# Placing the heads' rows: neighbouring rows against alternating rows

## Chip, cores and metric

The kernel runs on one core of a Trainium2 chip. The metric is the device time of one execution in microseconds. The five engines of the core work from queues of their own, each in order: PE (TensorE, matrix multiplies; PEld is its weight load), DVE (VectorE), ACT (ScalarE), POOL (GpSimd) and SP (SyncE, which here only issues DMAs). [...]

## The reference

A gated linear attention with a complex gate, then a mixture of experts in which each token goes to one expert. Shapes: q, k, v, a_re, a_im are (4, 8, 768, 48): batch, head, token, dimension.

```python
mag = np.sqrt(a_re * a_re + a_im * a_im)
scale = np.minimum(mag, 0.999) / (mag + 1e-06)
a_re_n, a_im_n = (a_re * scale, a_im * scale)
for t in range(S):
    ar, ai = (a_re_n[:, :, t, :, None], a_im_n[:, :, t, :, None])
    new_re = ar * S_re - ai * S_im
    new_im = ar * S_im + ai * S_re
    kv = np.einsum('bhd,bhe->bhde', k[:, :, t], v[:, :, t])
    S_re, S_im = (new_re + kv, new_im)
    y[:, :, t] = np.einsum('bhd,bhde->bhe', q[:, :, t], S_re)

x = y.transpose(0, 2, 1, 3).reshape(3072, 384)
logits = x @ w_gate                      # 8 experts
expert_idx = np.argmax(logits, axis=1)
gate_w = softmax(logits)[expert_idx]
for e in range(8):
    xe = x[expert_idx == e]
    out[expert_idx == e] = gate_w * (np.maximum(xe @ w1[e], 0.0) @ w2[e])
```

## The kernel before

**From gates to a matrix product.** The product of gates from one token to another is the exponential of a difference of running sums of logarithms, with an angle that is a difference of running sums too. So each q and k is multiplied by its own magnitude and by the cosine and the sine of its own angle, and q·k over the 96 rows "48 cosine products, 48 sine products" is the score. A chunk of 128 tokens is then done as ordinary causal attention inside the chunk plus a state carried from chunk to chunk.

**Two layouts.** The gates, queries and keys are worked on in 128 rows with three groups `g` along the row: `BLOCKS` (L25) lists which rows and groups hold which heads and dimensions. Heads 0 to 2 are rows 0 to 47 of the groups 0 to 2, heads 3 to 5 rows 48 to 95; heads 6 and 7 are cut: their dimensions 0 to 31 are rows 96 to 127 of the groups 0 and 1, their dimensions 32 to 47 rows 96 to 111 and 112 to 127 of group 2. The host lays the inputs out so (`_layout`, L797), so all 128 rows work in every elementwise instruction. The matrix multiplies want something else: for each head, 96 rows that hold part 0 (cosine) and part 1 (sine) of its 48 dimensions. That is the tile `hz` (two slots of 384 tokens, q and k of eight heads along the row, rows 96 to 127 zero).

**`front(u)`** (L273) does a unit of 128 to 384 tokens (`UNITS`, L27, ten of them): loads of gates (`AB`) and of q and k (`Z`) on SP (L292), logarithms and exponentials on ACT (L259), running sums as scans on DVE (L314, L325), sine and cosine on ACT, and four products on DVE into `zp`, [128 rows, part, q|k x group x token] (L337 to L345). Then ten DMAs copy `zp` to `hz` (L346 to L362): for each part and each block, rows of `zp` to the rows `part * D + d0` and following of `hz`. They are issued by SP, for the first unit four of them by ACT. There is one `zp`, so the next unit's products wait until these copies have read it.

**`chunk(b, c, full)`** (L369) does one chunk of 128 tokens out of `hz`: transposes of k on PE (L388) copied by ACT to `kt` (L390), scores (L395, `bank<-hz`), the causal mask on DVE into `am` (L399; shown as L172, the helper that issues it), the state's part (L407), the values (L414), the state's update (L422) and the turn to token rows (L430). `route` (L435) chooses experts, and POOL scatters the token rows to DRAM (L490). After all that the experts run (L608 to L670): weights loads on SP (L603, L605), token rows read back (L612), matrix multiplies L639 and L653.

**The order.** Up to the experts no order is written by hand. Each operation is added to a `Plan` (L46) with its engine, an assumed duration, the keys that it reads and writes, and for a DMA a latency `lat` and a wire time `wire`; `run` (L94) simulates the queues, and `order` (L142) tries 36 priorities and takes the shortest. The sequence of instructions in every engine's queue follows from these figures. For the copies into `hz` the wire time is the bytes at 0.213 MB per us (L361).

**The fallback.** If a check of the numbers' range fails at run time, a slow exact version (L686 to L791) runs in place of the result. It uses `BLOCKS` too (L715 to L723). With these inputs it doesn't run.

Of the kernel before, what the change touches and what calls it, by code (L numbers as in the profile page):

```python
# [12 lines left out]
AX = mybir.AxisListType.X  # L13
ALU = mybir.AluOpType
# [3 lines left out]
B, H, S, D = 4, 8, 768, 48  # L18
# [3 lines left out]
DT, FT = DM // 128, F // 128  # L22
G = 3

BLOCKS = ((0, 48, 0, 3, 0, 0), (48, 96, 0, 3, 3, 0), (96, 128, 0, 2, 6, 0), (96, 112, 2, 3, 6, 32), (112, 128, 2, 3, 7, 32))  # L25
TU = 384
UNITS = [(0, 0, 128), (0, 128, 384), (0, 384, 768)] + [(b, t, t + TU) for b in (1, 2) for t in (0, TU)] + [(3, 0, 384), (3, 384, 640), (3, 640, 768)]  # L27
NU = len(UNITS)
# [130 lines left out]
def gateloop_then_moe(ctx, tc, gates, qk, v, wg, w1, w2, out):  # L159
    nc = tc.nc  # L160
# [13 lines left out]
    def const(shape, nm, val=None, dt=FP32):  # L174
        t = consts.tile(shape, dt, name=nm)
        if val is not None:
            nc.gpsimd.memset(t, val)
        return t
# [13 lines left out]
    ident = const([128, 128], "ident")  # L192
# [26 lines left out]
    with ExitStack() as att:  # L219
        ap = att.enter_context(tc.tile_pool(name="ap", bufs=1))  # L220

        def buf(nm, n, shape, dt=FP32):
            return [ap.tile(shape, dt, name=f"{nm}{i}") for i in range(n)]
# [4 lines left out]
        zp, = buf("zp", 1, [128, 2, 2 * G * TU])  # L228
# [6 lines left out]
        hz = buf("hz", 2, [128, 2 * H * TU])  # L235
# [37 lines left out]
        def front(u):  # L273
            b, t0, t1 = UNITS[u]
            T = t1 - t0
# [5 lines left out]
            slot = (2 * b + t0 // TU) % 2  # L281
            sl = slice(0, T)
            a, im, c = bAB[s][:, 0, :, sl], bAB[s][:, 1, :, sl], bC[s][:, :, sl]
# [53 lines left out]
            for part, key, tr in ((1, Sk, si), (0, ("co",), co)):  # L337
                for x, xk, src in ((1, K, kk), (0, Q, qq)):
                    def f(part=part, tr=tr, x=x, src=src):
                        if T == TU:  # L340
                            tt(zp[:, part].rearrange("p (z g t) -> p z g t", z=2, g=G)[:, x], src, tr, ALU.mult)
                        else:
                            o = zp[:, part].rearrange("p (c z g t) -> p z g c t", z=2, g=G, t=128)[:, x, :, 0:nch]
                            tt(o, src.rearrange("p g (c t) -> p g c t", t=128), tr.rearrange("p g (c t) -> p g c t", t=128), ALU.mult)
                    P.add("DVE", dve2(n), f, (xk,) + tuple(key), (("zp", part, x),), port=True)  # L345
            for part in (1, 0):  # L346
                for p0, p1, g0, g1, h0, d0 in BLOCKS:
                    m, r0 = g1 - g0, part * D + d0
                    eng, dma = ("ACT", nc.scalar) if u == 0 and part == 0 and h0 else ("SP", nc.sync)

                    def f(dma=dma, p0=p0, p1=p1, g0=g0, g1=g1, h0=h0, r0=r0, m=m, part=part):
                        o, i = hz[slot][r0:r0 + p1 - p0], zp[p0:p1, part]
                        if T == TU:
                            o, i = o.rearrange("p (z x) -> p z x", z=2), i.rearrange("p (z x) -> p z x", z=2)
                            dma.dma_start(o[:, :, h0 * T:(h0 + m) * T], i[:, :, g0 * T:g1 * T])
                        else:
                            o = o.rearrange("p (c x) -> p c x", x=H * 128)[:, 2 * cl:2 * (cl + nch), h0 * 128:(h0 + m) * 128]
                            dma.dma_start(o, i.rearrange("p (c x) -> p c x", x=G * 128)[:, 0:2 * nch, g0 * 128:g1 * 128])
                    i = P.add(eng, 0.65, f,
                        (("zp", part, 0), ("zp", part, 1)), tuple(("h", slot, cl + x, h, part, d0) for x in range(nch) for h in range(h0, h0 + m)),  # L360
                        lat=1.6, wire=2 * (p1 - p0) * m * T * 4e-6 / 0.213)  # L361
                    moved.setdefault(u, []).append(i)  # L362

        def load_v(b, half):
# [147 lines left out]
        with tc.manual_schedule():  # L512
# [18 lines left out]
            for i in P.order():  # L531
                o = P.ops[i]
# [153 lines left out]
    with tc.If(flag[0] > 0, preferred_fallthrough_block=False), ExitStack() as fs:  # L686
# [4 lines left out]
        v_tok = v.rearrange("b c p (h w) -> (c p) b h w", h=H)  # L691
        x_tok = x_gen.rearrange("(b s) (h e) -> s h b e", b=B, h=H)
        with tc.For_i(0, S // TU) as hi, tc.For_i(0, TU, TB) as j0:
            i0 = hi * TU + j0
            a = fp.tile([128, 2, B, G, TB], FP32, name="fa")
            z_ = fp.tile([128, 2, B, G, TB], FP32, name="fqk")
            for o, src in ((a, gates), (z_, qk)):
                for u in range(2):
                    for b in range(B):
                        nc.sync.dma_start(o[:, u, b], src[b].rearrange("s p u g t -> p s u g t")[:, ds(hi, 1), u, :, ds(j0, TB)])  # L700
            M_ = B * G * TB
            sq = fp.tile([128, 2, M_], FP32, name="fsq")
            mag = fp.tile([128, M_], FP32, name="fmag")
            den = fp.tile([128, M_], FP32, name="fden")
            af = a.rearrange("p u b g t -> p u (b g t)")
            nc.scalar.activation(sq, af, func=ACT.Square)
            tt(mag, sq[:, 0, :], sq[:, 1, :], ALU.add)
            nc.scalar.activation(mag, mag, func=ACT.Sqrt)
            nc.vector.tensor_scalar_add(den, mag, 1e-6)
            nc.vector.reciprocal(den, den)  # L710
            nc.vector.scalar_tensor_tensor(out=den, in0=mag, scalar=0.999, in1=den, op0=ALU.min, op1=ALU.mult)
            tt(af, af, bc(den[:, None, :], [128, 2, M_]), ALU.mult)
            heads = fp.tile([128, G, H], FP32, name="heads")
            nc.gpsimd.memset(heads, 0.0)
            for p0, p1, g0, g1, h0, d0 in BLOCKS:  # L715
                for g in range(g0, g1):
                    nc.vector.tensor_reduce(mag[:, 0:1], ident[:, p0:p1], axis=AX, op=ALU.add)
                    tt(heads[:, g, h0 + g - g0:h0 + g - g0 + 1], heads[:, g, h0 + g - g0:h0 + g - g0 + 1], mag[:, 0:1], ALU.add)
            for t in range(TB):
                vt = fp.tile([128, G, B, D], FP32, name="vt")  # L720
                for p0, p1, g0, g1, h0, d0 in BLOCKS:
                    for g in range(g0, g1):
                        nc.sync.dma_start(vt[p0:p1, g], v_tok[ds(i0 + t, 1), :, h0 + g - g0].to_broadcast([p1 - p0, B, D]))  # L723

                def col(x, u):
                    return bc(x[:, u, :, :, t:t + 1].rearrange("p b g o -> p g b o"), shape)
                z = {}
                for x in range(2):
                    for y in range(2):
                        z[x, y] = fp.tile(shape, FP32, name=f"fz{x}{y}")  # L730
                        for g in range(G):
                            tt(z[x, y][:, g], state[:, x, g], col(a, y)[:, g], ALU.mult)
                kv = fp.tile(shape, FP32, name="kv")
                for g in range(G):
                    tt(kv[:, g], vt[:, g], col(z_, 1)[:, g], ALU.mult)
                tt(state[:, 0], z[0, 0], z[1, 1], ALU.subtract)
                tt(state[:, 1], z[0, 1], z[1, 0], ALU.add)
                tt(state[:, 0], state[:, 0], kv, ALU.add)
                for g in range(G):
                    tt(kv[:, g], state[:, 0, g], col(z_, 0)[:, g], ALU.mult)  # L740
                for g in range(G):
                    nc.tensor.matmul(bank[0][0:H, 0:B * D], lhsT=heads[:, g, :], rhs=kv[:, g].rearrange("p b e -> p (b e)"),
                                     start=(g == 0), stop=(g == G - 1))
                ys = fp.tile([H, B, D], FP32, name="ys")
                nc.vector.tensor_copy(ys.rearrange("h b e -> h (b e)"), bank[0][0:H, 0:B * D])
                for b in range(B):
                    nc.sync.dma_start(x_tok[ds(i0 + t, 1), :, b].rearrange("o h e -> (o h) e"), ys[:, b])
        with tc.For_i(0, NT, 1) as ti:
# [13 lines left out]
            m = fp.tile([128, 1], FP32, name="m")  # L762
# [34 lines left out]
def _layout(name, a):  # L797
    import numpy as _np
    if name in ('q', 'k', 'a_re', 'a_im'):
        z = _np.zeros((B, 128, G, S), a.dtype)  # L800
        for p0, p1, g0, g1, h0, d0 in BLOCKS:
            z[:, p0:p1, g0:g1] = a[:, h0:h0 + g1 - g0, :, d0:d0 + p1 - p0].transpose(0, 3, 1, 2)
        a = z.reshape(B, 128, G, S // TU, TU).transpose(0, 3, 1, 2, 4)
    elif name == 'v':
        a = a.transpose(0, 2, 1, 3).reshape(B, C, 128, DM)
    elif name == 'moe_w_gate':
        z = _np.zeros((128, 4, E), a.dtype)
        for h in range(H):
            z[64 * (h % 2):64 * (h % 2) + D, h // 2, :] = a[h * D:h * D + D]
        a = _np.concatenate([z.reshape(128, 4 * E), a.reshape(4, DT, 32, E).transpose(0, 2, 1, 3).reshape(128, DT * E)], axis=1)  # L810
    elif name == 'moe_w1':
        a = a.reshape(E, 4, DT, 32, F).transpose(0, 1, 3, 2, 4).reshape(E * 128, DT * F)
    else:
        a = a.reshape(E, FT, 128, DM).transpose(0, 2, 1, 3).reshape(E * 128, FT * DM)
    return _np.ascontiguousarray(a)
# [21 lines left out]
```

## Time and profile before

| | |
|---|---|
| median of 6 runs | 581.61 us (577.99 to 583.36) |
| profiled execution | 581.38 us, of which the span of instructions is 579.6 us |
| mean granted TensorE clock | 0.922 |
| PE busy | 476.6 us (82%), 2689 instructions |
| PEld | 322.1 us (56%) |
| DVE busy | 272.5 us (47%), 449 instructions |
| ACT busy | 187.1 us (32%) |
| POOL busy | 115.8 us (20%) |
| DMA | 86.15 MB in 48424 packets, mean 149 GB/s |
| copies `hz<-zp` | 100 issues: 96 by SP, 4 by ACT; 2.6 to 13.1 us from issue to landing, median 5.6 |

How to read the prediction's lines. A line of a stage gives its start and end, its length, then for each engine the busy microseconds and in brackets the number of instructions; then the share of full clock that TensorE was granted, the mean busy share of the 16 DMA engines (it can pass 1 slightly), and the GB/s that they moved. A line of the waits names who waited for whom, then the microseconds in total, the number of waits and the longest. A line of the timeline gives start, length, engine, line, operation, output and input, and in square brackets the idle time before it and what ended it. The shares over the whole span hide that there are two halves: attention up to about 262 us, in which all engines and the DMAs are in use, and the experts from about 280 us on, which are nearly all TensorE.

### The profile page before, as it was taken

To read this page: it belongs to the slowest core of one execution; us is meant where nothing else is said; L and a number is where in the kernel's file an instruction comes from. 1 tells how busy PE (TensorE), PEld (TensorE's weight loads), DVE (VectorE), ACT (ScalarE), POOL (GpSimd) and SP (SyncE) were. 2 spreads that over 40 slices of the span, in tenths; PEclk is the share of its full clock that TensorE was granted. 3 is DMA by queue.
4 is the path that set the end of the run, shared out by engine and by line. 5 is a ranking of instruction groups with operands and counts; after the bars stand their busy time and mean duration, and the time that the engine had idled before them with its cause. 6 is when DMAs were issued, how large, how long until landed. Compare 5 with 4: busy or idle time off the path is not lost. (4 is left out here: it accounts for less than half of the span.)

```text
span 579.6 us, 6981 instructions
## 1 busy us (share of the span) xinstructions
PE 476.6 (82%) x2689; PEld 322.1 (56%) x2689; DVE 272.5 (47%) x449; ACT 187.1 (32%) x261; POOL 115.8 (20%) x116
## 2 busy tenths in 40 slices
PE   0056639778978598991699999999999999999995
PEld 0055529668867487991355555555555555555552
DVE  7788978799998797742221202212022120211011
ACT  6666684668684665540011001000010000000000
POOL 6063111214610821503000002010020100202022
PEclk9975958898979598997699999999999999999999
DMA  8649494969899993787984504546042300401001
GB/s 273 155 170 256 121 207 134 243 180 242 225 255 215 230 207 75 173 341 243 289 145 121 155 15 146 147 135 168 16 152 109 124 15 14 149 0 32 1 36 34
DMA packets 48424, 86.15 MB, mean 149 GB/s; under 512 B 22512, under 2 KB 37904, under 8 KB 46336
## 3 DMA queue, kind: packets, MB, share of 16 engines
q1 hardware_dynamic: 43840, 75.19, 49.3%
q0 software_dynamic: 3328, 9.86, 4.7%
q10 hardware_dynamic: 1216, 0.59, 0.6%
q8 instruction: 23, 0.38, 0.3%
q14 instruction: 17, 0.14, 0.1%
HBM read 54.32 MB, written 13.21 MB: 117 GB/s over the span
## 5 line engine op out<-in xcount | busy, mean ns | idle before, releaser
L639 PE MATMUL bank<-xrt,w1b 128*128 128x448 f32 x384 | 149.5, 546 | 9.3 <-DVE xrt L624 9.3
L653 PE MATMUL bank<-w2b,ht 128*128 128x384 f32 x384 | 127.7, 487 | 0.0
L639 PEld LDWEIGHTS bank<-xrt,w1b 128*128 128x128 f32 x384 | 73.8, 193 | 80.0 <-issue 66.4
L395 PE MATMUL bank<-hz 128*128 128x128 f32 x384 | 65.0, 326 | 59.5 <-DMA hz<-zp 48.5
L653 PEld LDWEIGHTS bank<-w2b,ht 128*128 128x128 f32 x384 | 72.6, 190 | 54.0 <-issue 8.7
L645 ACT ACTIVATE ht<-bank 128x448 f32<-128x448 f32 x32 | 17.4, 543 | 262.7 <-PE bank L639 262.7
L395 PEld LDWEIGHTS bank<-hz 128*128 128x128 f32 x384 | 57.5, 231 | 64.4 <-DVE lend L296 28.7
L586 POOL DMA_INDIRECT out_dram<-yo,gi x24 | 23.5, 978 | 276.7 <-DVE yo L597 243.1
L642 DVE TENSOR_SCALAR ht<-bank 128x448 f32<-128x448 f32 x32 | 19.9, 623 | 114.1 <-PE bank L639 114.1
L597 DVE TENSOR_SCALAR yo<-bank,gi 128x384 f32<-128x384 f32 x24 | 14.8, 618 | 100.0 <-PE bank L653 100.0
L172 DVE TENSOR_TENSOR zp<-Z,cs 128x1152 f32<-128x1152 f32 (+2 forms) x40 | 44.4, 1149 | 0.3
L172 DVE TENSOR_TENSOR am<-bank,causal 128x512 f32<-128x512 f32 x48 | 32.3, 682 | 23.3 <-PE bank L395 23.2
L172 POOL TENSOR_TENSOR AB<-AB,C 128x1152 f32<-128x1152 f32 (+2 forms) x9 | 20.4, 2271 | 91.0 <-ACT C L259 50.9
L414 PE MATMUL bank<-am,v 128*48 128x128 f32 x384 | 28.9, 291 | 11.4 <-DVE am L172 11.2
L490 POOL DMA_INDIRECT xs_hbm<-xg,slot x24 | 29.4, 1224 | 31.3 <-DVE z L172 13.5
L172 POOL TENSOR_TENSOR Z<-Z,AB 128x1152 f32<-128x1152 f32 (+2 forms) x9 | 21.3, 2372 | 59.0 <-ACT AB L259 58.8
L430 PE MATMUL bank<-turn,yt 128*128 128x104 f32 x192 | 28.6, 295 | 4.9 <-ACT yt L418 4.5
L535 ACT ACT_TABLE_LOAD x25 | 32.1, 1283 | 1.2 <-PEq L825 0.8
L422 PE MATMUL bank<-v,kt 128*96 128x48 f32 x320 | 31.6, 253 | 0.0
L422 PEld LDWEIGHTS bank<-v,kt 128*96 128x96 f32 x320 | 30.1, 170 | 2.0 <-issue 2.0
L430 PEld LDWEIGHTS bank<-turn,yt 128*128 128x128 f32 x192 | 24.9, 203 | 8.4 <-ACT yt L418 5.8
L414 PEld LDWEIGHTS bank<-am,v 128*48 128x48 f32 x384 | 21.7, 130 | 13.9 <-DVE am L172 12.1
(111 smaller groups left out, 465.2 us busy)
## 6 DMA issues: line engine op xcount, KB each, us to landing
w1b<-in_w_dram SPq DMA_DIRECT2D x8, 1536.0 KB, 6.8
w2b<-in_w_dram SPq DMA_DIRECT2D x8, 1536.0 KB, 6.8
hz<-zp SPq DMA_DIRECT2D x24, 432.0 KB, 8.0
AB<-in_gates_dram SPq DMA_DIRECT2D x12, 576.0 KB, 5.5
Z<-in_qk_dram SPq DMA_DIRECT2D x12, 576.0 KB, 5.0
xb<-xs_hbm SPq DMA_DIRECT2D x30, 168.0 KB, 6.0
v<-in_v_dram SPq DMA_DIRECT2D x8, 576.0 KB, 7.0
xs_hbm<-empty SPq DMA_DIRECT2D x3, 836.0 KB, 11.3
```

The source lines that it names most:

```text
L172: (eng or nc.vector).tensor_tensor(out=o, in0=a, in1=b, op=op)
L395: nc.tensor.matmul(SC[hf][:, (h % 4) * 128:(h % 4) * 128 + 128], lhsT=hk[:, h], rhs=hq[:, h], start=True, stop=True)
L414: nc.tensor.matmul(YT[ps, (h // 2) * 128:(h // 2) * 128 + 128], lhsT=V[:, cl, h * D:h * D + D], rhs=am[2 * par + hf][:, h % 4, :], start=( ...
L422: nc.tensor.matmul(ST[0:96, h * D:h * D + D], lhsT=kt[par][:, h * 96:h * 96 + 96], rhs=V[:, cl, h * D:h * D + D], start=(c == 0 and h == 0 ...
L430: nc.tensor.matmul(XT[:, p * 104:p * 104 + 104], lhsT=yt[par][:, p * 128:p * 128 + 128], rhs=turn[:, p, :], start=True, stop=True)
L490: i = nc.gpsimd.indirect_dma_start(out=xs_hbm[:, :], out_offset=bass.IndirectOffsetOnAxis(ap=R[slot][:, c:c + 1], axis=0), in_=xg[:, (g0 + ...
L535: nc.scalar.preload_act_table_set("natural_log_exp_and_others" if P.cur == "LE" else "trig_and_small")
L586: i = nc.gpsimd.indirect_dma_start(out=out[:, :], out_offset=bass.IndirectOffsetOnAxis(ap=index, axis=0), in_=y, in_offset=None, bounds_ch ...
L639: nc.tensor.matmul(HB[hb][:, 0:CAP], lhsT=w1b[ws][:, c:c + 128], rhs=xrt[s][:, d, :], start=(d == 0), stop=(d == DT - 1))
L642: M.add("DVE", 0.6, lambda f_=f_, hb=hb: nc.vector.tensor_scalar_max(ht[s][:, f_, :], HB[hb][:, 0:CAP], 0.0), (("H", hb),), (("ht", s, f_),))
L645: M.add("ACT", 0.6, lambda f_=f_, hb=hb: nc.scalar.activation(ht[s][:, f_, :], HB[hb][:, 0:CAP], func=ACT.Relu), (("H", hb),), (("ht", s, ...
L653: nc.tensor.matmul(OB[ob][:, 0:DM], lhsT=ht[s][:, f_, j * 128:j * 128 + 128], rhs=w2b[ws][:, f_ * DM:f_ * DM + DM], start=(f_ == 0), stop= ...
```

## The change

`BLOCKS` holds slices now. Heads 0 to 2 take the even rows 0, 2, ..., 94 of the gates and queries and heads 3 to 5 the odd rows 1, 3, ..., 95, where each had 48 neighbouring rows. In `hz`, part 0 goes to the even rows and part 1 to the odd rows of 0 to 95: dimension `d` of a head is in rows `2 d + part`, where it was in row `48 part + d`. Rows 96 to 127 of the gates and queries hold what they held. The planner's wire time for these copies is computed with 0.34 MB per us in place of 0.213. The host's layout and the fallback follow the same table.

```diff
-BLOCKS = ((0, 48, 0, 3, 0, 0), (48, 96, 0, 3, 3, 0), (96, 128, 0, 2, 6, 0), (96, 112, 2, 3, 6, 32), (112, 128, 2, 3, 7, 32))
+BLOCKS = ((slice(0, 95, 2), 48, 0, 3, 0, 0), (slice(1, 96, 2), 48, 0, 3, 3, 0), (slice(96, 128), 32, 0, 2, 6, 0),
+          (slice(96, 112), 16, 2, 3, 6, 32), (slice(112, 128), 16, 2, 3, 7, 32))
...
             for part in (1, 0):
-                for p0, p1, g0, g1, h0, d0 in BLOCKS:
-                    m, r0 = g1 - g0, part * D + d0
+                for ps, np, g0, g1, h0, d0 in BLOCKS:
+                    m, r0 = g1 - g0, 2 * d0 + part
                     eng, dma = ("ACT", nc.scalar) if u == 0 and part == 0 and h0 else ("SP", nc.sync)
 
-                    def f(dma=dma, p0=p0, p1=p1, g0=g0, g1=g1, h0=h0, r0=r0, m=m, part=part):
-                        o, i = hz[slot][r0:r0 + p1 - p0], zp[p0:p1, part]
+                    def f(dma=dma, ps=ps, np=np, g0=g0, g1=g1, h0=h0, r0=r0, m=m, part=part):
+                        o, i = hz[slot][r0:r0 + 2 * np - 1:2], zp[ps, part]
...
-                        lat=1.6, wire=2 * (p1 - p0) * m * T * 4e-6 / 0.213)
+                        lat=1.6, wire=2 * np * m * T * 4e-6 / 0.34)
...
-            for p0, p1, g0, g1, h0, d0 in BLOCKS:
+            for ps, np, g0, g1, h0, d0 in BLOCKS:
                 for g in range(g0, g1):
-                    nc.vector.tensor_reduce(mag[:, 0:1], ident[:, p0:p1], axis=AX, op=ALU.add)
+                    nc.vector.tensor_reduce(mag[:, 0:1], ident[:, ps], axis=AX, op=ALU.add)
...
-                        nc.sync.dma_start(vt[p0:p1, g], v_tok[ds(i0 + t, 1), :, h0 + g - g0].to_broadcast([p1 - p0, B, D]))
+                        nc.sync.dma_start(vt[ps, g], v_tok[ds(i0 + t, 1), :, h0 + g - g0].to_broadcast([np, B, D]))
...
-        for p0, p1, g0, g1, h0, d0 in BLOCKS:
-            z[:, p0:p1, g0:g1] = a[:, h0:h0 + g1 - g0, :, d0:d0 + p1 - p0].transpose(0, 3, 1, 2)
+        for ps, np, g0, g1, h0, d0 in BLOCKS:
+            z[:, ps, g0:g1] = a[:, h0:h0 + g1 - g0, :, d0:d0 + np].transpose(0, 3, 1, 2)
```

More of the change, by code (lines that the diff above doesn't have):

```diff
@@ L800, in _layout @@
         z = _np.zeros((B, 128, G, S), a.dtype)
-        for p0, p1, g0, g1, h0, d0 in BLOCKS:
-            z[:, p0:p1, g0:g1] = a[:, h0:h0 + g1 - g0, :, d0:d0 + p1 - p0].transpose(0, 3, 1, 2)
+        for ps, np, g0, g1, h0, d0 in BLOCKS:
+            z[:, ps, g0:g1] = a[:, h0:h0 + g1 - g0, :, d0:d0 + np].transpose(0, 3, 1, 2)
         a = z.reshape(B, 128, G, S // TU, TU).transpose(0, 3, 1, 2, 4)
```

## The prediction, made before the changed kernel was run

> **What bounds the kernel now.** I read the stages first: the busy time of each engine in stretches cut where the large hz transfers begin.
>
> ```profile
> core 0: us, PE busy (x) PEld busy (x) DVE busy (x) ACT busy (x) POOL busy (x), PEclk, DMA share, GB/s
> 30.00:65.00 35.00, 24.16 (x194) 21.50 (x194) 31.57 (x34) 23.87 (x28) 13.57 (x7) 0.71 0.61 172
> 65.00:96.00 31.00, 16.15 (x125) 14.49 (x125) 24.19 (x29) 20.78 (x23) 5.24 (x2) 0.67 0.78 181
> 96.00:122.00 26.00, 21.31 (x215) 19.46 (x214) 22.89 (x34) 19.66 (x26) 5.25 (x2) 0.93 0.83 213
> 122.00:148.00 26.00, 21.95 (x239) 20.18 (x238) 25.79 (x33) 18.12 (x27) 12.17 (x6) 0.93 0.87 210
> 148.00:176.00 28.00, 22.59 (x222) 20.63 (x221) 27.76 (x35) 20.14 (x27) 8.52 (x6) 0.88 1.00 251
> 176.00:205.00 29.00, 20.15 (x194) 18.32 (x194) 23.70 (x34) 15.88 (x22) 15.26 (x10) 0.76 1.02 225
> 228.00:262.00 34.00, 33.98 (x385) 31.28 (x383) 20.77 (x70) 15.64 (x30) 9.88 (x12) 0.97 0.80 253
> 280.40:579.60 299.20, 292.68 (x896) 155.24 (x896) 48.73 (x88) 17.38 (x32) 27.38 (x28) 0.99 0.32 94
> ```
>
> The experts (280.4 to the end) are TensorE's, 292.7 of 299.2 us, and use no hz: the change can move only when they start. Before 228 VectorE is the fullest engine, with nothing free from 122 to 176. From 228 to 262 TensorE has no pause, and in fact its backlog begins at 197, where the hz of the seventh unit (unit 6 of 0 to 9) has landed: from 197 to 262 it works 62.2 of 65 us. So the question is what delays VectorE up to about 183 (zp of unit 6 done) and that transfer up to 197. The waits of VectorE from 30 to 228, then two of TensorE's in the timeline around 197:
>
> ```profile
> DVE am L172 <- PE bank L395: 20.7, 12, 3.4
> ```
> ```profile
> 194.42 1.62 PE L395 MATMUL bank<-hz 128*128 128x128 f32 x6 [5.94 <-DMA hz<-zp]
> 197.35 0.76 PE L395 MATMUL bank<-hz 128*128 128x128 f32 x2 [1.30 <-DMA hz<-zp]
> ```
>
> VectorE's idle time there is 22.9 us (198.0 less 175.1 busy), and 20.7 of it is the causal multiply waiting for the scores of L395, whose own wait, where the profile names it, is for hz. How fast does hz move? Four windows inside one unit's ten transfers and the load after them:
>
> ```profile
> 98.50:100.00 1.50, 1.50 (x19) 1.47 (x17) 1.50 (x3) 1.12 (x2) 0.70 (x1) 1.00 0.79 144
> 100.50:102.00 1.50, 1.48 (x28) 1.22 (x24) 1.50 (x5) 0.10 (x1) 1.44 (x1) 1.00 0.94 259
> 104.50:108.00 3.50, 2.47 (x28) 1.97 (x27) 3.47 (x6) 3.43 (x5) 0.00 (x0) 1.00 1.02 169
> 112.20:117.00 4.80, 4.80 (x37) 4.49 (x37) 3.30 (x8) 4.77 (x5) 0.00 (x0) 0.78 1.04 399
> ```
>
> The last column is GB/s, the one before it the DMA engines' share. The engines look equally full (1.02 and 1.04) at 169 GB/s for hz copies and at 399 GB/s for 128-row loads: the copies are held up by something other than a lack of work. And copies of the same shape (432 KB, 48 rows) go at 144 and at 259. The trace does not name rows; taken in the order of the code, the first is rows 0-47 to 48-95 and the second rows 48-95 to 48-95.
>
> **The change, part by part.** *Counts.* Ten transfers per unit stay ten, with the same bytes and pieces, on the same queues; matrix multiplies, copies and VectorE's work keep their number and shapes (rows of a contraction are permuted, in q, k, kt and sb alike). That costs 0. The fallback (L715 to L723) does not run: the trace has no instruction of those lines.
>
> *The four 432 KB transfers of a unit of 384 tokens* (part 0 and 1, heads 0-2 and 3-5) read and write every second row of 0 to 95 instead of 48 neighbouring ones. 4 x 432 KB is 1.77 MB. Now: the window 123 to 134, ten hz transfers and nearly nothing else, shows 190 GB/s, so 9.3 us. Bounds: not faster, saving 0 (a loss per byte has no row that would make it: the pieces stay 4608 bytes); at the load's 399 GB/s 4.4 us, saving 4.9. I take 259 GB/s, the best row of the same shape, because the new rows are spread at least as widely as 48-95: 6.8 us, **saving 2.5 us** per unit of 384, and 1.7 for one of 256.
>
> *The six small ones* (192 KB, twice 48 KB, per part) still read rows 96-127; only their targets spread. I take 0, and at most 1 us: 0.59 MB at 190 GB/s is 3.1 us, at 259 2.3.
>
> [...]
>
> *Where the saving counts.* Unit 1 (256 tokens, stage 30-65): the multiply waits 4.7 us in two waits, so 1.7 counts. Unit 2 (65-96): 6.1 in three, longest 3.4, so 2.5. Unit 3 (96-122): 3.0 in three, of which only the first, 1.55, ends with a landing; the others follow TensorE at half clock. 1.5. Units 4 and 5 (122-176): 0, covered by VectorE's own 25.8 of 26 and 27.8 of 28 us; if that cover went, 2.5 each. Unit 6: its transfer ends the wait before 197, 2.5 whole. Behind 197 nothing: TensorE is full, and unit 7's hz, of which it now waits 1.1 us, comes earlier by the same amounts. Sum: 1.7 + 2.5 + 1.5 + 2.5 = **8.2 us**.
>
> *The planner's wire figure*, 0.213 to 0.34 MB per us, moves no byte, but the orders of all queues are computed from it. 2.36 MB per unit were put at 11.1 us (11.7 to issue on SP in two stages) and are now put at 6.9: 4.2 sooner, where I expect 2.5. An instruction placed for the early landing stands 1.7 us in VectorE's in-order queue, and everything behind it, the next unit's scans and zp, waits too. Where VectorE has idle time this is already in the waits above; in units 4 and 5 it has none: 2 x 1.7 = 3.4, of which I count half, 1.7, since not each late landing meets the head of the queue. Bounds of the re-ordering: a gain of 3 (the gate loads queued on SP behind hz come up to 5.6 us late in 176-205 and would be issued sooner) to a loss of 8.4 (4.2 twice).
>
> Forecast: 8.2 less 1.7 is 6.5. The profiled execution took 581.4 us, its span 579.6 and 1.8 around it, against a median of 581.6; from the latter, **575.1**.
>
> **The rivals.** (1) *Hidden anyway*, no change: the transfers do run faster, but the multiply then waits for scores that TensorE, idle and at half clock (matrix multiplies of 583 ns beside 275), brings no sooner, or for ACT's next exponential; of the four places only unit 6's 2.5 stays, less the 1.7: about 581. For it: only one of unit 3's three waits ends at a landing. Against: unit 6's 5.9 us wait is a plain one for hz. (2) *Slower: the order believes a rate that the copies don't reach.* Place: VectorE's queue in units 4 and 5 (122-176). Price: (4.2 - S) per unit, S being the true saving; the gain side is 8.2/2.5 = 3.3 S. With the full price at both units it is slower from S = 1.6 down (copies under 230 GB/s), with half of it from S = 1.0 (213). At S = 0, that is when row numbers are not what holds the copies up, it is 8.4 us: 590. For it: the small transfers keep their source rows, and from 175 to 181 hz shares the engines with the 2.5 MB of L523. (3) *Larger gain*: S = 4.9. Unit 1 3.3, unit 2 4.9, unit 3 1.5, unit 6 4.9, 14.6 together, no late order left: 567.
>
> **How the numbers follow.** A measurement of this kernel tells about 0.5% (2.9 us) from no change. Forecast (S near 2.5, gain 3 to 11) 0.44; larger gain 0.17; hidden 0.17; slower 0.22. The forecast's own range is 571 to 579. Low end 566, just past the larger gain; the upper end leaves out the worse half of the slower case: 586. Faster: 0.44 + 0.17 = 0.61, plus 0.01 of the hidden case; same 0.17: the hidden case less that, and 0.01 of the slower; slower 0.21.
>
> **What would show it.** Right: in stretches where hz alone moves, over 240 GB/s instead of 144 to 190; ten hz transfers leave SP in 8 to 10 us instead of 11.7; VectorE's wait for L395 falls from 20.7 to about 13; the experts start near 274 instead of 280.4, and last 299 us as before. Wrong in the mechanism: the same GB/s in those stretches. Wrong in where it counts: faster copies, but the experts start at 280 with a new wait (ACT, or the multiply) in VectorE's list. Rival 2: the wait of the multiply grows in the stages 122 to 176, which now show almost no idle time. A change of the experts' own length would mean that I misread the reach of the change.

## The result and the profile after

The changed kernel takes 584.81 us (582.01 to 590.77 over 24 runs), the kernel before, timed beside it, 581.0. The ratio is 1.007 with a 95% interval of 1.005 to 1.0089: **slower by 0.7%**, where 575.1 was forecast. The profiled execution took 586.77 us, its span is 585.0.

First the stages, cut where large `hz` transfers begin; the cuts come later than before because the stages do.

```profile
core 0: us, PE busy (x) PEld busy (x) DVE busy (x) ACT busy (x) POOL busy (x), PEclk, DMA share, GB/s
30.00:62.00 32.00, 22.05 (x176) 20.17 (x176) 27.96 (x32) 24.88 (x29) 11.75 (x6) 0.88 0.64 200
62.00:93.00 31.00, 15.50 (x93) 14.01 (x94) 27.98 (x27) 21.65 (x23) 6.17 (x2) 0.52 0.59 172
118.00:150.00 32.00, 28.33 (x266) 25.13 (x265) 30.50 (x41) 24.08 (x32) 6.47 (x3) 0.82 0.65 181
182.00:214.00 32.00, 22.64 (x240) 20.69 (x240) 26.85 (x43) 17.72 (x27) 11.82 (x10) 0.84 0.93 217
286.50:585.00 298.50, 292.14 (x896) 155.11 (x896) 48.63 (x88) 17.42 (x32) 27.23 (x28) 0.99 0.32 95
```

The experts last 298.5 us (299.2 before) but start at 286.5 instead of 280.4. So the loss lies in the attention half, and it is 6 us there. The stretch 62 to 93 shows TensorE half idle at half clock while VectorE is at 28 of 31.

Next, how fast the copies go. These are stretches of `after` inside the ten transfers of units 3, 5 and 7 (by the packet sizes in the trace the first holds the end of a gate load too, the others some packets of loads and scatters):

```profile
102.00:109.00 7.00, 3.73 (x39) 3.25 (x38) 6.90 (x7) 3.34 (x4) 1.47 (x1) 1.00 0.96 284
150.00:160.00 10.00, 10.00 (x110) 8.87 (x106) 9.67 (x15) 6.97 (x10) 6.22 (x4) 1.00 0.98 255
212.00:222.00 10.00, 9.99 (x124) 9.26 (x123) 8.41 (x12) 9.16 (x13) 3.39 (x3) 1.00 0.92 251
```

Before, copies showed 144 to 259 GB/s, and 190 over a whole unit. So the transfers did become faster. Two lines of the page agree: the queue that carries them is busy for 45.5% of the span (49.3% before) with the same packets and bytes, and a large transfer lands 6.2 us after its issue, not 8.0. First the kernel before, then the changed one:

```profile
q1 hardware_dynamic: 43840, 75.19, 49.3%
...
hz<-zp SPq DMA_DIRECT2D x24, 432.0 KB, 8.0
```
```profile
q1 hardware_dynamic: 43840, 75.19, 45.5%
...
hz<-zp SPq DMA_DIRECT2D x24, 432.0 KB, 6.2
```

Yet VectorE's wait for the scores, which was to fall from 20.7 us to 13, stayed (30 to 240 us; total, number of waits, longest):

```profile
DVE am L173 <- PE bank L396: 20.0, 12, 3.9
DVE cs L326 <- ACT AB L260: 2.9, 2, 1.6
```

And TensorE's wait for unit 6's `hz`, 5.9 us before, is 9.3 here, and it ends 9 us later on the clock:

```profile
203.47 2.24 PE L396 MATMUL bank<-hz 128*128 128x128 f32 x8 [9.29 <-DMA hz<-zp]
```

Faster copies and later work: the two halves of the change have to be taken apart.

### The profile page after: what moved, and what is told of

The parts are those of the page before. It is cut to its first block, busy times and chain, and to the rows that moved or that the text cites. A ratio compares the mean times of both kernels' runs of the same rounds, so it can differ in the third digit from the quotient of the medians.

```text
span 585.0 us, 6967 instructions
## 1 busy us (share of the span) xinstructions
PE 479.8 (82%) x2689; PEld 324.0 (55%) x2689; DVE 278.2 (48%) x449; ACT 195.5 (33%) x267; POOL 113.4 (19%) x116
## 3 DMA queue, kind: packets, MB, share of 16 engines
q1 hardware_dynamic: 43840, 75.19, 45.5%
## 5 line engine op out<-in xcount | busy, mean ns | idle before, releaser
L396 PE MATMUL bank<-hz 128*128 128x128 f32 x384 | 62.8, 319 | 60.1 <-DMA hz<-zp 60.1
L646 ACT ACTIVATE ht<-bank 128x448 f32<-128x448 f32 x32 | 17.4, 544 | 265.3 <-PE bank L640 265.3
L396 PEld LDWEIGHTS bank<-hz 128*128 128x128 f32 x384 | 56.3, 227 | 63.5 <-issue 53.1
L173 DVE TENSOR_TENSOR zp<-Z,cs 128x1152 f32<-128x1152 f32 (+2 forms) x40 | 47.1, 1215 | 0.2
L173 DVE TENSOR_TENSOR am<-bank,causal 128x512 f32<-128x512 f32 x48 | 32.5, 683 | 20.5 <-PE bank L396 20.4
L173 POOL TENSOR_TENSOR Z<-Z,AB 128x1152 f32<-128x1152 f32 (+2 forms) x9 | 23.9, 2660 | 82.1 <-ACT AB L260 74.6
L415 PE MATMUL bank<-am,v 128*48 128x128 f32 x384 | 31.4, 302 | 4.2 <-DVE am L173 4.2
L491 POOL DMA_INDIRECT xs_hbm<-xg,slot x24 | 25.6, 1066 | 46.5 <-DVE ok L552 12.9
L173 POOL TENSOR_TENSOR AB<-AB,C 128x1152 f32<-128x1152 f32 (+2 forms) x9 | 22.6, 2514 | 58.9 <-ACT C L260 57.9
L389 PE MATMUL bank<-ident,hz 96*128 96x96 f32 x160 | 25.2, 297 | 9.5 <-DMA hz<-zp 9.5
L431 PE MATMUL bank<-turn,yt 128*128 128x104 f32 x192 | 30.3, 307 | 1.4 <-ACT yt L419 1.4
L431 PEld LDWEIGHTS bank<-turn,yt 128*128 128x128 f32 x192 | 26.6, 214 | 4.9 <-issue 2.8
```

Source lines behind the costliest of these rows:

```text
L173: (eng or nc.vector).tensor_tensor(out=o, in0=a, in1=b, op=op)
L389: nc.tensor.transpose(KT[hf][:, (h % 4) * 96:(h % 4) * 96 + 96], hk[0:96, h], ident[0:96, 0:96])
L396: nc.tensor.matmul(SC[hf][:, (h % 4) * 128:(h % 4) * 128 + 128], lhsT=hk[:, h], rhs=hq[:, h], start=True, stop=True)
L415: nc.tensor.matmul(YT[ps, (h // 2) * 128:(h // 2) * 128 + 128], lhsT=V[:, cl, h * D:h * D + D], rhs=am[2 * par + hf][:, h % 4, :], start=( ...
L431: nc.tensor.matmul(XT[:, p * 104:p * 104 + 104], lhsT=yt[par][:, p * 128:p * 128 + 128], rhs=turn[:, p, :], start=True, stop=True)
L491: i = nc.gpsimd.indirect_dma_start(out=xs_hbm[:, :], out_offset=bass.IndirectOffsetOnAxis(ap=R[slot][:, c:c + 1], axis=0), in_=xg[:, (g0 + ...
```

## The experiments

All times below are medians, and each ratio is to the kernel before on the same chip (580 to 581 us; 585 on the chip of e9 to e12).

**One half at a time.** The changed kernel has two edits that need not go together: which rows (of SBUF, the on-chip memory) hold the heads, and the planner's figure, from which the order of all queues follows.

```diff
# e1_rows_only: the new rows, the old figure
-                        lat=1.6, wire=2 * np * m * T * 4e-6 / 0.34)
+                        lat=1.6, wire=2 * np * m * T * 4e-6 / 0.213)
# e2_figure_only: the kernel before, the new figure
-                        lat=1.6, wire=2 * (p1 - p0) * m * T * 4e-6 / 0.213)
+                        lat=1.6, wire=2 * (p1 - p0) * m * T * 4e-6 / 0.34)
```

> The new rows with the planner's old figure, 0.213: every queue has the instructions of the kernel before in the same order, so this is the effect of the rows alone. Theory (the copies gain what was forecast, and the new order loses it): copies at 230 to 260 GB/s where the kernel before has 190, experts start 3 to 7 us before 280.4, 574 to 578 us. Rival 1 (faster copies are hidden by other waits): the same GB/s as in the theory, but 580 to 582 us. Rival 2 (alternating rows themselves cost): over 584 us.

> The old rows with the planner's new figure, 0.34: every queue has the order of the changed kernel, over copies at the old rate. Theory (the order is what costs): the changed kernel's 584.8 plus the gain of the rows, 588 to 594 us, with 31 table loads on ACT and copies at about 190 GB/s. Rival 1 (copies hidden): about 585, as the changed kernel. Rival 2 (the rows cost, the order is harmless): 579 to 582.

Measured: the rows alone 567.98 us, ratio 0.9772 (0.9744 to 0.98); the figure alone 607.08 us, 1.0461 (1.0413 to 1.0509). So the rows save 12 to 13 us (12.1 by the medians, 13 by the ratio), more than expected, and the new order costs 27 on the old rows, where at most 14 was expected, and 17 (584.8 less 568.0) on the new ones. The kernel with the rows alone is the best of this study. Its windows (units 3 and 6, then the experts) and its wait for the scores from 30 to 228 us:

```profile
92.00:103.00 11.00, 9.49 (x114) 8.45 (x113) 10.97 (x16) 7.17 (x12) 2.64 (x1) 1.00 0.97 227
170.50:179.00 8.50, 8.50 (x106) 7.51 (x106) 7.90 (x11) 3.72 (x8) 0.00 (x0) 1.00 0.97 243
268.00:567.10 299.10, 292.63 (x896) 155.28 (x896) 48.73 (x88) 17.39 (x32) 27.38 (x28) 0.99 0.31 94
```
```profile
DVE am L172 <- PE bank L395: 7.2, 8, 1.7
```

This is the picture that was forecast, only more of it: the wait falls to 7.2 and the experts start at 268. For units 3 and 6 SP issues the ten copies in the 8 to 10 us that were named as a sign (with loads and other writes beside them, units 2, 4, 5 and 7 take 11 to 13). Unit 6 in the kernel before, then in e1:

```profile
175.39 15.14 SPq L355 DMA_DIRECT2D hz<-zp  x10
```
```profile
169.71 9.55 SPq L355 DMA_DIRECT2D hz<-zp  x10
```

The wait for the scores with the figure alone, from 28 to 265 us, is five times as long:

```profile
DVE am L173 <- PE bank L396: 36.7, 14, 10.3
```

**Which side's rows.** The new layout alternates both what the copies read (`zp`) and what they write (`hz`).

```diff
# e5_targets_only, on e1: hz alternates, gates and queries as before
-BLOCKS = ((slice(0, 95, 2), 48, 0, 3, 0, 0), (slice(1, 96, 2), 48, 0, 3, 3, 0), ...
+BLOCKS = ((slice(0, 48), 48, 0, 3, 0, 0), (slice(48, 96), 48, 0, 3, 3, 0), ...
# e6_sources_only, on e1: gates and queries alternate, hz as before
-                    m, r0 = g1 - g0, 2 * d0 + part
+                    m, r0 = g1 - g0, part * D + d0
...
-                        o, i = hz[slot][r0:r0 + 2 * np - 1:2], zp[ps, part]
+                        o, i = hz[slot][r0:r0 + np], zp[ps, part]
```

> Half of the row change, in the order of the kernel before (figure 0.213): heads 0 to 2 and 3 to 5 keep neighbouring rows in the gates and queries (the side that is read), and only the targets in hz alternate. Rows alone, both sides, were 568.0 us. Theory that the read and the written rows each limit a copy: copies of heads 0-2 stay at the old rate, those of heads 3-5 speed up; 572 to 577 us. Rival 1, only the written rows matter: 567 to 570. Rival 2, only the read rows matter: 579 to 582.

> The other half, in the order of the kernel before: heads 0 to 2 and 3 to 5 alternate in the gates and queries, and hz keeps part 0 in rows 0 to 47 and part 1 in rows 48 to 95. Theory that both sides limit: copies of part 0 stay at the old rate, those of part 1 speed up; 572 to 577 us. Rival 1, only the written rows matter: 579 to 582. Rival 2, only the read rows matter: 567 to 570.

Measured: targets 573.08 us, 0.99 (0.9851 to 0.9949); sources 574.4 us, 0.9886 (0.9835 to 0.9938). Each side brings about half, 6 to 7 us, with four runs each and an interval of some 3 us either way, and the sum of the two ratios' gains, 12.4 us, is near the 13 of both. Neither end of a copy alone holds it up.

**The figure.** If the order is bad because 0.34 is more than the copies reach, a truer figure must do well. With the new rows and nothing else changed than the number in the `wire=` line:

```diff
-                        lat=1.6, wire=2 * np * m * T * 4e-6 / 0.34)
+                        lat=1.6, wire=2 * np * m * T * 4e-6 / 0.25)
```

> The changed kernel with 0.27 MB per us in the planner's figure in place of 0.34; the copies of the changed kernel were measured at about 245 to 258. Its order has 25 table loads on ACT, as the kernel before, where the changed kernel has 31. Theory that the table loads of the order are what costs (6 of 1.28 us each): 574 to 579 us. Theory that the figure's distance from the true rate costs: also 574 to 579. Rival (any new order is as bad, because the old one was found by trials on the chip): 583 to 587.

> The changed kernel with 0.25 MB per us, the figure nearest to the measured rate; its order has 33 table loads on ACT. Theory that table loads are what costs: 584 to 589 us. Theory that the figure's distance from the true rate costs: 574 to 578 us, the fastest of the orders. Rival (any new order): 583 to 587, as with 0.27.

> The changed kernel with 0.30 MB per us in the planner's figure. With the new rows 0.213 gave 568.0, 0.25 570.0, 0.27 571.8 and 0.34 584.8. Theory that a figure above the true rate (about 0.245) costs the more the further it is above: between the last two, 574 to 580 us. Rival, that 0.34 happened upon one bad order out of many: 567 to 573, as the others. Table loads on ACT in this order are 33, as with 0.25.

> The changed kernel with 0.45 MB per us, still further above the true rate (about 0.245). Theory that a figure above the truth costs in itself, and the more the further: 585 to 600 us. Rival, that each figure throws up one order of many and only its collisions count: anywhere between 567 and 590, with no trend.

> The new rows with 0.17 MB per us, well below the true rate. Theory that only a figure above the truth costs much (an instruction placed late finds its data there, one placed early stops a queue): 567 to 574 us. Rival, that any distance from the truth costs alike: 578 to 586. Rival, that 0.213 happened to be a good order: anywhere between 567 and 590.

| figure, MB per us | us | ratio (95%) | experts start, us | VectorE idle up to the last `zp`, us |
|---|---|---|---|---|
| 0.17 | 572.78 | 0.9857 (0.9821 to 0.9894) | 272.2 | 17.6 |
| 0.213 | 567.98 | 0.9772 (0.9744 to 0.98) | 268.0 | 10.6 |
| 0.25 | 570.0 | 0.9825 (0.9791 to 0.9858) | 269.7 | 17.8 |
| 0.27 | 571.82 | 0.9836 (0.9801 to 0.9872) | 270.3 | 14.5 |
| 0.30 | 583.6 | 1.0052 (1.0024 to 1.0081) | 284.8 | 26.5 |
| 0.34 | 584.81 | 1.007 (1.005 to 1.0089) | 286.5 | 24.7 |
| 0.45 | 595.07 | 1.0159 (1.0082 to 1.0237) | 296.0 | 36.7 |

The last column is summed from 25 us on, without pauses under some 40 ns, and is good to about 1 us. The figure 0.45 ran on the chip where before takes 585, so its ratio is the number to compare. The copies show 227 to 255 GB/s in most stretches read. All figures up to 0.27 give a fast order and all from 0.30 a slow one, with a step of 12 us between 0.27 and 0.30. That step was in neither expectation of 0.30 (574 to 580, or 567 to 573). Another suspicion falls here: `after` has 31 table loads on ACT of 1.28 us each against 25 before, but the fast kernel with 0.25 has 33.

The trend fits "an order pays for a belief above the truth". But it fits as well "the planner's high figures happen to give poor orders". On the old rows the copies run near 190 GB/s, so there 0.25 is above the truth by nearly a third:

```diff
# e15_old_rows_025: the kernel before, with
-                        lat=1.6, wire=2 * (p1 - p0) * m * T * 4e-6 / 0.213)
+                        lat=1.6, wire=2 * (p1 - p0) * m * T * 4e-6 / 0.25)
```

> The old rows with the figure 0.25: the order of e4_figure_025, which took 570.0 over the fast copies, laid over copies of about 190 GB/s. Theory that a figure above the true rate costs: more than the 12 us that slow copies cost in the order of 0.213, so 586 to 595 us. Rival, that this order is good in itself: 570 plus 12, 580 to 584.

Measured: 583.34 us, 1.0015 (0.9979 to 1.0051). That belief cost next to nothing, as the rival said (580 to 584). It speaks against the belief as the whole cause.

**Where in the queue.** The timeline of VectorE and SP shows what the order of 0.34 does to unit 2. In `after` the four products into `zp` (two sine, then two cosine) are spread, with the next unit's scans between them; SP can copy only half at a time (five transfers of ten).

```profile
62.05 2.63 DVE L173 TENSOR_TENSOR zp<-Z,cs 128x1152 f32<-128x1152 f32 x2
...
66.42 5.17 DVE L315 TENSOR_TENSOR_SCAN D<-AB,lend,C 128x384 f32<-128x384 f32 x3
71.51 1.89 DVE L326 TENSOR_TENSOR_SCAN cs<-bank,tend,AB 128x384 f32<-128x384 f32 x2
...
73.64 1.36 DVE L173 TENSOR_TENSOR zp<-Z,cs 128x1152 f32<-128x1152 f32 x1
74.92 3.76 DVE L305 CUSTOM_DVE_ANT_0 C<-AB 128x1152 f32<-128x1152 f32 x1
...
78.61 1.35 DVE L173 TENSOR_TENSOR zp<-Z,cs 128x1152 f32<-128x1152 f32 x1
```
```profile
64.71 4.66 SPq L356 DMA_DIRECT2D hz<-zp  x5
79.99 5.07 SPq L356 DMA_DIRECT2D hz<-zp  x5
```

With the old order on the same rows the last product ends at 69.5 instead of 80.0, and the custom instruction takes 1.33 us. SP copies five and five there too, but the second five begin at 69.9 instead of 80.0.

```profile
59.35 3.89 DVE L172 TENSOR_TENSOR zp<-Z,cs 128x1152 f32<-128x1152 f32 x3
63.35 1.02 DVE L325 TENSOR_TENSOR_SCAN cs<-bank,tend,AB 128x384 f32<-128x384 f32 x1
...
68.17 1.35 DVE L172 TENSOR_TENSOR zp<-Z,cs 128x1152 f32<-128x1152 f32 x1
...
71.15 1.33 DVE L304 CUSTOM_DVE_ANT_0 C<-AB 128x1152 f32<-128x1152 f32 x1
```

Scores need both halves of `hz`, so a late cosine half makes the early sine half useless. This can be tried: keep the order of `after` and bring the cosine products and their copies forward, behind the sine ones, in units 2 to 7 (e8), or in units 2, 4 and 6 alone (e9 and e14, the same kernel).

```diff
+def joined(P, prod, moved):
+    seq = P.order()
+    for u in (2, 4, 6):
...
+        at = max(rest.index(x) for x in prod[u, 1] + [d for z in cos for d in dep(z)])
+        rest[at + 1:at + 1] = cos
...
```

A second suspect is in unit 6: the three DMAs that clear rows of `xs_hbm` (L524, 2.5 MB) share the engines with its copies (SP takes 17.4 us to issue those ten). In e10 the three are issued behind unit 6's copies; e11 does both. e13 is the changed kernel once more, beside e14 on the same chip.

> The changed kernel (figure 0.34) with one thing put right by hand in its order: in the units 2 to 7 the two cosine products of VectorE follow the two sine products, and the five copies of part 0 follow those of part 1 on SP, instead of coming up to 15 us later behind scans of the next unit and behind loads. TensorE, ACT and POOL keep their order. Theory that the late second half of the products and copies is most of what the order costs: 571 to 577 us. Rival, that the order costs through masks placed too early in VectorE's queue wherever they stand, or through ACT's six more table loads: 581 to 588.

> The changed kernel (figure 0.34) with the joining of e8_join in the units 2, 4 and 6 alone, where every moved instruction comes earlier than it did: cosine products right behind the sine products on VectorE, copies of part 0 right behind those of part 1 on SP. If the late second half is a real part of the cost: 575 to 580 us. If e8_join's reading holds (a unit that is copied earlier only puts off the next one's scans, and VectorE's total stays): 582 to 586.

> The changed kernel (figure 0.34) with one thing moved on SP: the three DMAs that write 2.5 MB of empty rows (L524) are issued behind the copies of unit 6, not ahead of them; the four compute engines keep their order. In the changed kernel SP stood 8.2 us at them, waiting for the scatters of batch 0, and their packets ran until 189.9 us over unit 6's copies (181 to 199); with 0.213 they were through at 170.2, when those copies began. Theory that this collision is a large part of the cost: copies of unit 6 issued in about 10 us and not 17.4, 575 to 580 us. Rival, that the order's other stalls come first: 582 to 586.

> Both of the last two edits on the changed kernel (figure 0.34). If the two account for the cost of the order: 567 to 573 us, as with the figures 0.213 to 0.27. If only the empty rows count: as e10_clear_later within 2 us. If neither: 581 to 586.

> The changed kernel once more, beside e14_join_three on the same chip; ratio to the kernel before 1.005 to 1.009 by the first measurement.

> The kernel of e9_join_three again, to set it against the changed kernel on one chip. Theory that the late second half is about half of what the order costs (17 us): 6 to 10 us below e13_after, ratio to the kernel before 0.990 to 0.997. Rival, that the 0.993 of the last chip was its scatter: within 2 us of e13_after.

Measured: e8 583.11 us, 1.0045 (1.0023 to 1.0067); in it part of batch 1 is computed from the wrong keys, because in its order the load that refills a `Z` buffer for unit 5 (issued at 93.2 us) stands ahead of unit 3's cosine product that still reads it. e9 582.51, 0.9932 (0.989 to 0.9973), on the chip where before takes 585.28. e10 585.83, 0.9988 (0.9943 to 1.0033), and e11 586.08, 1.0011 (0.997 to 1.0051), on that chip too. e13 584.72, 1.0052 (1.0025 to 1.0078); e14 579.36, 0.9973 (0.9941 to 1.0005). So joining the halves returns 5.4 us (584.72 less 579.36) of the 17, shown side by side, a little under the 6 to 10 that were expected. It is no remedy for every unit: joined in all six, e8 is at most 1.5 us better than `after` by the ratios, in the range that its rival named (581 to 588), though its misplaced load may have cost it something. Moving the clearing DMAs shortens the issue of unit 6's copies from 17.4 to 9.6 us (e11). Whether it gains time stays unclear: the changed kernel wasn't timed on that chip, and e9 and e14, one kernel, differ by 0.004 between the two chips. With the join it isn't added to the join's gain (e11 586.08, e9 582.51 on one chip); moved, the 2.5 MB runs from 188 to 202 us in e11, just ahead of unit 7's copies, which SP begins to issue at 202.

**The belief made true.** The last pair keeps both orders and shortens the copies of units 2 and 4 to 7 until 0.34 is about right for them.

```diff
# e17_cut_034 on after, e18_cut_0213 on e1
+        for h in (2, 5):
+            nc.vector.memset(hz[1][0:96].rearrange("p (z h t) -> p z h t", z=2, h=H)[:, :, h], 0.0)
...
-                            dma.dma_start(o[:, :, h0 * T:(h0 + m) * T], i[:, :, g0 * T:g1 * T])
+                            k = 2 if m == 3 and u in (2, 4, 5, 6, 7) else m
+                            dma.dma_start(o[:, :, h0 * T:(h0 + k) * T], i[:, :, g0 * T:(g0 + k) * T])
```

> The changed kernel's order (figure 0.34) with copies made shorter: in units 2, 4, 5, 6 and 7 the four large copies leave out heads 2 and 5, 288 KB each in place of 432, so a unit moves 1.77 MB and not 2.36. Those heads' scores are computed from zeros or older data, that part of the computation is changed. Every queue holds the same instructions in the same order, with one clearing of hz added at the start. At some 240 GB/s 1.77 MB take 7.4 us, where the planner was told 6.9: the order's belief is nearly true. Theory A (an order made for copies faster than the real ones pays for it): the cost of the order goes, at most 6 us above the run with figure 0.213 and the same short copies, 565 to 572. Rival B (this order is bad in itself, whatever the copies take): still at least 12 us above that run, 577 to 583. Between, both have a share.

> The same short copies under the order of figure 0.213 (the kernel with the new rows alone). Both theories: its copies had stopped being what its VectorE waits for, so little changes, 563 to 568. It is the reference for the run with figure 0.34: theory A has that run at most 6 us above this one, rival B at least 12.

Measured: 579.51 us, 0.9993 (0.9964 to 1.0023), against 568.88, 0.9782 (0.974 to 0.9824). The gap shrinks from 17 us to 10.6 by the medians, between the two theories' bounds; by the ratios (0.9993 less 0.9782) it is 12, which is rival B's bound. So the order itself keeps at least the larger share, and how much more is not settled. Shorter copies do nothing for the order of 0.213 (567.98 with whole copies) and bring 5 us to that of 0.34. VectorE's wait from 25 to 250 us, in e17 and then in e18:

```profile
DVE am L173 <- PE bank L399: 13.9, 10, 6.4
```
```profile
DVE am L172 <- PE bank L398: 10.0, 11, 1.8
```

VectorE's time from 25 us to the end of the last product into `zp`, summed from the traces (idle without pauses under some 40 ns, good to about 1 us; busy is the rest), shows which part went and which stayed (us):

| kernel | last `zp` ends | idle | of it the mask's waits | busy |
|---|---|---|---|---|
| before | 241.3 | 24.0 | 21.4 | 192.3 |
| e1, rows alone | 229.6 | 10.6 | 8.7 | 193.9 |
| after | 250.3 | 24.7 | 20.4 | 200.6 |
| e2, figure alone | 270.2 | 45.0 | 38.5 | 200.2 |
| e17, 0.34, short copies | 242.4 | 17.2 | 13.9 | 200.2 |
| e18, 0.213, short copies | 230.6 | 10.2 | 8.6 | 195.4 |
| e14, after with joined halves | 241.7 | 19.8 | 15.2 | 196.9 |

Between `after` and e17 only the idle time falls, by 7.5 us; the busy time is 200 us under the order of 0.34 on old rows, new rows and short copies alike, and 192 to 195 under that of 0.213. So the waits depend on how fast the copies are, and 5 to 8 us more of VectorE work ahead of the last product belong to the order itself.

Only a part of that is longer work. Over the whole program VectorE (DVE) has the same 449 instructions in e1 and in `after`, and is busy with them 3.7 us longer (their lengths added up differ by 1.3 us, 297.9 and 299.2; neighbours also overlap less):

```profile
PE 475.5 (84%) x2689; PEld 321.0 (57%) x2689; DVE 274.5 (48%) x449; ACT 187.2 (33%) x261; POOL 115.9 (20%) x116
```
```profile
PE 479.8 (82%) x2689; PEld 324.0 (55%) x2689; DVE 278.2 (48%) x449; ACT 195.5 (33%) x267; POOL 113.4 (19%) x116
```

Most of the other 3 us of the 6.7 in the table come from where the order puts things: 267 instructions start between 25 us and the end of the last product in `after`, 261 in e1, and behind it 60.0 us of work are left instead of 62.2.

## Why the prediction was wrong

*What bounds the kernel: right for the experts, short for the attention.* The experts kept 298.1 to 299.8 us in every profile, so only their start moved. But it isn't VectorE up to unit 6 alone that decides that start: of the 11.7 us that e1's last product comes sooner, 6.0 arise behind unit 6, where TensorE, taken as full, waits for VectorE in e1 (4.7 us at 189.7).

*The rows: right in mechanism, under-sized, 8.2 us forecast and 12 to 13 measured (580.1 to 568.0 on one chip; 13 by the ratio).* The large copies were put at 259 GB/s; all ten of a unit show 227 and 243 in e1, and SP is through with them some 2 us sooner (9.61 us for unit 3, 11.78 before), so the rate was not put too low. The sum up to unit 6 was good: 1.7 + 2.5 + 1.5 is 5.7, and in e1 the last product of unit 6 ends at 172.2 instead of 177.9, 5.7 us sooner. That it fits to the tenth is partly luck: the last product of unit 4 is 7.0 us sooner, and 1.3 of that is lost again. Behind unit 6, 2.5 us were counted for unit 6's transfer and "nothing" further on, since TensorE was full there. In fact the last product of unit 9 ends 11.7 us sooner (229.6, 241.3): 6.0 behind unit 6, not 2.5. Unit 6's copies also no longer share the engines with the clearing DMAs (those are done at 170.2, and the copies leave SP from 169.7; before, they ran until 182.7, over copies issued from 175.4), and their issue shrinks by 5.6 us, from 15.14 to 9.55. The prediction saw that sharing but gave it no saving. What the targets alone bring, ratio 0.99 beside 0.9886 for the sources, shows that the written rows count as much as the read ones; the six small transfers, whose targets alone spread and which were put at 0, may hold part of the rest. That wasn't tried by itself.

*The planner's wire figure: the step that failed.* A cost of 1.7 us ("of which I count half, 1.7") with an outer bound of 8.4 stood against 17 measured on the new rows and 27 on the old ones. Three things were wrong in it:

- The price. It took the new order to be the old one with instructions placed at most 4.2 us too early. But one figure re-orders all queues. Compared with e1, the last product of `after` ends 20.7 us later: VectorE is idle 14.1 us longer, of which 11.7 is the mask waiting for scores, and does 6.7 us more work before it, 3.7 because it is busy longer with the whole program and most of the rest because more instructions stand ahead. The 5.6 us of late gate loads, from which its bound of a gain was taken, are two waits together, the longest 4.9.
- The place. Units 4 and 5 were named. Unit 2 is already 10.5 us late (80.0, 69.5), and after unit 6 it is 14.2 (186.4, 172.2).
- The reason. The belief above the real rate is part of it: making it true returned 17 - 10.6 = 6 us by the medians (5 by the ratios), bringing the cosine halves of three units forward 5.4 (the two may overlap). The other 10.6 to 12 us stay with this order when the copies are that short: against e18 the last product still ends 11.8 us later, 4.8 of it more work ahead of it and 7.0 waits. No term of the sum and no rival held more work for VectorE.

*The rivals.* Rival 2 had the sign and, in its belief, a third of the cause; its own price, (4.2 - S) a unit with S near 2, would have been 4.4 us for two units against a gain of 3.3 S, 6.6, so still a win. Rival 1 is out: the same copies under the old order gain 12 to 13. Rival 3, the larger gain, named 567 for the rows, and the rows alone take 568.0; that is luck, since it needed copies at 399 GB/s and they show 227 and 243.

*What the rows show.* Copies over alternating rows show 227 and 243 GB/s in e1, with the DMA engines' share at 0.97; over neighbouring rows a whole unit went at 190, its copies out of rows 0 to 47 at 144 and 169 (rows by the order of the code). The prediction's reason for a faster copy, rows spread at least as widely as 48 to 95, agrees with that in direction; no run shows how a row's number sets the rate.

*What stays open.* Why VectorE is busy 3.7 us longer under the order of 0.34. Instructions stretched beside POOL's are seen under both orders, and no run took that overlap away. Nor is it settled which of its placements keeps the remaining 7 us of waits. With 0.30 the busy time is 196.4 and with 0.45 195.8, so their cost (idle 26.5 and 36.7 us) is of the other kind.

## What to carry to other kernels

A change that moves data faster and also tells a scheduler so is two changes: run each alone, since here one saved 12 to 13 us and the other cost 17. A figure in a planner is an input to a search that re-orders everything, so its effect can't be bounded by the size of the figure's error; try a few values around the rate that the trace shows, 0.17 to 0.27 here, and keep the one that runs best. Where a copy on chip goes far slower than a load with equally full DMA engines (here 169 GB/s beside 399, at shares of 1.02 and 1.04), look at which rows it touches, on both ends.

## What was not expected of the hardware

- Row numbers alone, with bytes, packets and queues the same (75.19 MB in 43840 packets on q1 in both kernels), moved these copies from 190 GB/s to 227 and 243 (e1), and the read and the written side contributed about alike (ratios 0.9886 and 0.99, together 0.9772).
- VectorE's instructions are not of fixed length. Three scans into `D` that take 2.83 us in e1 took 5.17 in `after`, and the custom instruction 3.76 against 1.33, each with a multiply of POOL in the same stretch:

```profile
67.06 2.80 POOL L173 TENSOR_TENSOR AB<-AB,C 128x1152 f32<-128x1152 f32 x1 [10.67 <-ACT C L260]
74.10 3.37 POOL L173 TENSOR_TENSOR Z<-Z,AB 128x1152 f32<-128x1152 f32 x1 [4.24 <-ACT AB L260]
```

Under the old order others are stretched: the custom instruction at 31 us takes 2.70 in e1, and 1.34 in `after`. In both kernels every VectorE instruction that takes over 0.3 us more than the shortest of its form shares at least 58% of its time with work of POOL. There are 16 in e1, 23.9 us over the shortest in all, and 14 in `after`, 25.0 us, so the new order stretches other instructions and hardly more. That POOL holds them up is inferred from the overlap; no run separated the two, and most instructions beside POOL aren't longer: in e1 two scans from `bank` took 1.92 us beside a multiply of POOL, and 1.89 in `after` without one.
